# The last residual of a decode kernel moved from VectorE to TensorE and ScalarE

## The chip, the cores and the metric

The kernel runs on one core of one Trainium2 chip. The metric is the device time of one execution in microseconds (us). A profile of one execution shows, for each engine (PE is TensorE, PEld its weight loads, DVE is VectorE, ACT is ScalarE, POOL is GpSimd, SP is SyncE), what ran when. Its span reaches from the first to the last instruction of the program; the time of the execution is a little longer than the span.

## What is computed

One token goes through an attention block over a key and value cache and then through a small MLP block. Cut to what matters:

```
h   = x + attention(layernorm(x), k_cache, v_cache, wq) @ wo   # 32 heads, 8 key/value heads, 16384 keys of 128
b   = layernorm(h)
x1  = b + hs          # hs comes from h's neighbours 1 and 2 tokens away; with one token it is zero
out = h + x1 + gelu(layernorm(x1) @ w3) @ w4                   # w3: 512 x 1792, w4: 1792 x 512
```

So x1 is layernorm(h), and the result is 512 numbers in bf16. `h + x1` is the residual of the title; the kernel calls it `xsum`.

## The kernel before, in words

The work is written as a list of operations, each with the names that it reads and writes, and `Program` (L25) turns the list into instructions for each engine with semaphore waits between them. Every engine works off its operations in the order in which they are written. All large loads are issued by SP, and so they land in the order of their issue: `wq`, then keys and values of four pairs of heads (`kb`, `vb`), then `wo` in three pieces (`WO`, L359, rows 0-15, 16-27, 28-31 of its 32), `w3` in two pieces, and `w4` in four (`W4`, L362: of its 14 chunks 0-3, 4-8, 9-12 and 13).

A loop over the four pairs computes scores, softmax and the values' sums (L727 to L744). TensorE runs it as a real loop of instructions (`_tensor`, L158): its code is one copy of the body, with branches back. VectorE's code is written out in full (`_vector`, L143).

Behind the loop comes the tail, which the change touches:

- `o_b` (L760) is the attention's result. The 32 matmuls with `wo` follow (L766). Where the second piece of `wo` begins, at `r_ == 16`, stands `unread(4)`: one matmul of 128 x 512 whose output nobody reads, run four times in a loop on TensorE (L505; the loop's branch is at L338).
- The result goes through a sum over partitions, gets `x` added and becomes `hr`, which is `h` laid out over 128 partitions x 128 (the 32 partitions of block q all hold columns 128q to 128q+127). Row sums, variances and two inverse roots give the two layernorms' factors; one root runs on VectorE, the other on GpSimd.
- `hc` (L780, ScalarE) goes into the 16 matmuls with `w3` (L786), ScalarE takes Gelu (L798), VectorE transposes the result into `hcol` in two halves (L802).
- GpSimd makes `xs`, which is x1, and `xsum = hr + xs` (L793, L795).
- 14 chunks of four matmuls each (L810) multiply `hcol` by `w4` and add up in `n_ps[:, 0:128]`, a PSUM tile of 128 x 128 in fp32. The four matmuls of a chunk write the four strips of 32 partitions.
- VectorE adds `n_ps` and `xsum` into `fin`, in bf16 (L815). SP writes rows 0, 32, 64 and 96 of `fin`, 256 B each, to the output (L817) and waits for that (L819).

Two operations of the tail have no function, `dve(None, ...)` at L805 and `pe(None)` at L808. Each stands for a branch that never goes back (L154 and L344): VectorE waits until the second piece of `w4` has landed and then runs its branch; TensorE runs its branch after the fourth chunk of `w4`. For both a branch hint was marked at the start of the program (L146, L223). The code behind the branch is a block of its own (`ve_on`, `pe_on`).

`_tensor` writes each operation with `times` outside the main loop as a loop block of its own (L330 to L341): here that is `unread(4)` alone.

`ident_f` is a 128 x 128 identity in fp32, made at the start.

Of the kernel before, what the change touches and what calls it, by code (L numbers as in the profile page):

```python
# [9 lines left out]
ALU = mybir.AluOpType  # L10
ACTF = mybir.ActivationFunctionType
# [347 lines left out]
WO = ((0, 16), (16, 28), (28, 32))  # L359
VP = 2  # L360
W3 = ((0, 2), (2, 4))
W4 = ((0, 4), (4, 9), (9, 13), (13, 14))  # L362
# [13 lines left out]
def bass_sequential_preLN__gqa_block_cached__mixer_s_mlp__decode_kernel(  # L376
# [13 lines left out]
    with ExitStack() as ctx:  # L390
# [18 lines left out]
        ident_f = sb("ident_f", [128, 128], FP32)  # L409
# [35 lines left out]
        xsum = sb("xsum", [128, 128], FP32)  # L445
# [3 lines left out]
        fin = sb("fin", [128, 128], BF16)  # L449
# [13 lines left out]
        m_ps, n_ps = mn_ps[:, 0:256], mn_ps[:, 256:512]  # L463
# [28 lines left out]
        def dve(fn, r=(), w=(), bank=()):  # L492
            return P.op("DVE", fn, r, w, bank)

        def act(fn, r=(), w=(), bank=()):
            return P.op("ACT", fn, r, w, bank)
# [4 lines left out]
        def pe(fn, r=(), w=(), bank=(), also=()):  # L501

            return P.op("PE", fn, r, w, bank, also=also)

        def unread(times):  # L505
            field = qb[:, :, :, :].rearrange("p a j q -> p (a j q)")
            P.op("PE", lambda e: e.matmul(O_ps[1][:, :], field[:, 0:128], field[:, 0:512], start=True, stop=True),  # L507
                 r=["qb"], bank=[("O", 1)], times=times)

        def piece(cuts, m):  # L510
            return [lo <= m < hi for lo, hi in cuts].index(True)

        def copies(col, n):

            return col.to_broadcast([col.shape[0], n])
# [38 lines left out]
        def inverse_root(i, n, by, beside):  # L554
# [9 lines left out]
            for m in range(3):  # L564
# [22 lines left out]
            r=["ident", "x4"], w=["quarter"])  # L587
        pe(lambda e: e.matmul(O_ps[0][:, 0:128], quarter[:, :, :].rearrange("p q u -> p (q u)"), x4[:, :],  # L588
                              start=True, stop=True), r=["quarter"], w=[("O", 0)], bank=[("O", 0)])
# [9 lines left out]
            r=["ident_f"], w=["row32"])  # L599
        dve(lambda e: e.tensor_reduce(maskdd[:, :], ident_f[:, :].rearrange("p (n d) -> p d n", d=4), AX.X, ALU.add),  # L600
            r=["ident_f"], w=["maskdd"])
# [6 lines left out]
        for z, m, key, mk in ((zo, rowgh, "zo", "rowgh"), (zd, maskgh, "zd", "maskgh")):  # L608
# [5 lines left out]
            r=["hT", (("st", 0), 0), (("st", 0), 6)] + [("v", x) for x in range(VP)], w=["xn"])  # L614
# [3 lines left out]
        for i, key in enumerate(keys):  # L618
            P.part("query", i)
            for k in range(NCH):  # L620
                pe(lambda e, k=k: e.matmul(row[:, bass.ds(P.b + P.b0, 512)], copies(xn[:, k:k + 1], 128),  # L621
                                           wq_k[:, k, bass.ds(P.c + P.c0, REP * DH)], start=(k == 0), stop=(k == NCH - 1)),
                   r=["xn"], also=[("v", x) for x in range(VP)], w=["n" if key == "mn" else key], bank=[key])
        P.part()
        for g in range(2):
            half = banks[64 * g:64 * g + 64, PAIRS * g:PAIRS * g + PAIRS, :].rearrange("p j c -> p (j c)")
            for b in range(2):
# [3 lines left out]
                    r=["n" if x == "mn" else x for x in keys[PAIRS * g:PAIRS * g + PAIRS]], w=["qcol"],  # L631
                    bank=keys[PAIRS * g:PAIRS * g + PAIRS])
# [121 lines left out]
        for n, (lo, hi) in enumerate(W4):  # L754
# [4 lines left out]
            r=["o_m"], w=["o_f"])  # L759
        dve(lambda e: e.tensor_copy(o_b[:, :], o_f[:, :]), r=["o_f", ("r", 0, 0)], w=["o_b"])  # L760

        for r_ in range(32):
            q = r_ % 4
            if r_ == WO[1][0]:
                unread(4)
            pe(lambda e, r_=r_, q=q: e.matmul(O_ps[0][32 * q:32 * q + 32, :], copies(o_b[:, r_:r_ + 1], 32),  # L766
                                              wo_sb[:, r_ * D:(r_ + 1) * D], start=(r_ < 4), stop=(r_ >= 28)),
               r=["o_b"] + [("r", 0, n) for n in (piece(WO, r_),) if n], w=[("O", 0)], bank=[("O", 0)])
        h_ps, hkey = banks[:, 6, :], "spare0"
        for n in range(2):  # L770
            dve(lambda e, n=n: e.tensor_copy(osum[:, 256 * n:256 * n + 256], O_ps[0][:, 256 * n:256 * n + 256]),
                r=[("O", 0)], w=[("osum", n)], bank=[("O", 0)])
        for q in range(4):
            pe(lambda e, q=q: e.matmul(h_ps[32 * q:32 * q + 32, 0:128], copies(row32[:, 0:1], 32),
                                       osum[:, q * 128:(q + 1) * 128], start=True, stop=True),
               r=[("osum", q // 2), "row32"], w=[hkey], bank=[hkey])
# [4 lines left out]
            r=["hT", (S, 0)] + [("r", 1, 0)], w=["hc"])  # L781


        for k in range(NCH):
            for q in range(4):
                pe(lambda e, k=k, q=q: e.matmul(s_ps[32 * q:32 * q + 32, 0, 0:FQ], hc[:, k, :],  # L786
                                                w3_sb[:, k, q * FQ:(q + 1) * FQ], start=(k == 0), stop=(k == NCH - 1)),
                   r=["hc"] + [("r", 1, n) for n in (piece(W3, k),) if n], w=[("s", 0)], bank=[("s", 0)])
# [5 lines left out]
            r=["hr", (S, 0), (S, 6)], w=["xs"])  # L794
# [11 lines left out]
        for m in range(NHC):  # L806
            if m == W4[1][0]:
                pe(None)  # L808
            for o in range(4):
                pe(lambda e, m=m, o=o: e.matmul(  # L810
                    n_ps[32 * o:32 * o + 32, 0:128], hcol[:, m, :], w4_sb[:, m, o * 128:(o + 1) * 128],
                    start=(m == 0), stop=(m == NHC - 1),
                    skip_group_check=True),
                   r=[("hcol", 2 * m // NHC)] + [("r", 1, len(W3) + n) for n in (piece(W4, m),) if n], w=["n"], bank=["mn"])
        dve(lambda e: e.tensor_tensor(fin[:, :], n_ps[:, 0:128], xsum[:, :], ALU.add), r=["n", "xsum"], w=["fin"],  # L815
            bank=["mn"])
        P.op("SP", lambda e: e.dma_start(out[0, 0:1, :].rearrange("o (q j) -> (o q) j", q=4), fin[0:128:32, :]),  # L817
             r=["fin"], w=["out"], dma="out")
        P.op("SP", lambda e: e.nop(), r=["out"])  # L819
# [31 lines left out]
```

## Time and profile before

| | |
|---|---|
| median of 3 runs | 192.34 us (192.22 to 192.51) |
| profiled execution | 192.24 us |
| its span | 190.3 us |
| granted TensorE clock, mean of the span | 0.86 of full speed |
| busy in the span | TensorE 125.7 us, VectorE 117.9 us, ScalarE 9.2 us, GpSimd 7.4 us |
| read from memory | 79.17 MB, 416 GB/s over the span |

How to read it: in a group of instructions, `out<-in` are the program's names, `x36` a count, and times in brackets are idle time of that engine just before, with what ended it. "L810" is line 810 of the kernel. The chain that ended last goes back from the last instruction to what released each step. Of 190.3 us, DMA has 66% of that chain, VectorE 15% and TensorE 14%. Matmuls are pipelined, so their ends are modelled. PEclk is the granted clock of TensorE as a share of full speed.

### The profile page before, as it was taken

The page shows a single profiled execution, that of the slowest core. Times are in us where ns is not written, and L with a number is a line of the kernel's source. Part 1 is how long each engine was busy: PE and PEld are TensorE (multiplying, and loading weights), DVE is VectorE, ACT ScalarE, POOL GpSimd, SP SyncE. Part 2 cuts the span into 40 slices and gives each one's busy share as a digit, 9 for nine tenths or more (in the row PEclk, how much of TensorE's full clock was granted, in tenths as well). Part 3 has the DMA queues.
Part 4 walks back from the last instruction along what each step waited for, and adds up shares of the span by engine and source line. Part 5 has one row for each costly group of instructions (what it writes and reads, how often), then busy time and mean ns, then how long its engine had stood idle before and what let it go on. Part 6 is the DMA issues. An engine that isn't in the chain of part 4 may idle for free.

```text
span 190.3 us, 2315 instructions
## 1 busy us (share of the span) xinstructions
PE 125.7 (66%) x733; PEld 48.5 (25%) x733; DVE 117.9 (62%) x152; ACT 9.2 (5%) x16; POOL 7.4 (4%) x16
## 2 busy tenths in 40 slices
PE   0119709997770599964944989658359996865552
PEld 0103303442230233321311433213113332321131
DVE  6740799995523989845049989450479895522270
ACT  3000000000200000011000000020000000500030
POOL 7100000000000000000000000000000000000050
PEclk9999995899999579998585899996858999799755
DMA  6999999999999999997999999889999999999991
GB/s 221 441 441 441 441 441 441 441 441 441 399 413 420 420 551 441 441 441 331 441 441 441 551 399 399 386 379 420 441 441 441 441 441 441 441 386 395 423 408 46
DMA packets 3330, 79.20 MB, mean 416 GB/s; under 512 B 384, under 2 KB 512, under 8 KB 1280
## 3 DMA queue, kind: packets, MB, share of 16 engines
q1 hardware_dynamic: 3320, 79.17, 97.1%
q8 instruction: 1, 0.02, 0.0%
q14 instruction: 1, 0.01, 0.0%
q10 hardware_dynamic: 8, 0.00, 0.0%
HBM read 79.17 MB, written 0.00 MB: 416 GB/s over the span
## 4 chain that ended last, share of the span: by engine, by line
DMA 66%; DVE 15%; PE 14%; issue 2%; SPq 1%; DVEq 0%
DMA kb<-in_A_k_cache_dram 45%; DMA kb<-in_B_w_dram 14%; DVE kt L644 14%; PE banks L661 9%; DMA vb<-in_A_wq_dram 6%; PE banks L621 5%; SPq L467 1%; DVE qcol L628 1%; PE banks L655 1%; DVE qb L635 0%; PE banks L810 0%; DVE xn L612 0%; DVE fin L815 0%; SPq L139 0%; DVEq L139 0%
## 5 line engine op out<-in xcount | busy, mean ns | idle before, releaser
L644 DVE STREAM_TRANSPOSE kt<-kb 128x2048 int32<-128x2048 int32 (+1 forms) x37 | 71.3, 1989 | 6.9 <-DMA kb<-in_A_k_cache_dram 5.3
L661 PE MATMUL banks<-kt,qn 128*128 x256 | 68.9, 416 | 0.9 <-DVE kt L644 0.2
L661 PEld LDWEIGHTS banks<-kt,qn 128*128 x256 | 26.5, 104 | 41.4 <-issue 23.8
L697 PE MATMUL banks<-vb,pt 128*32 128x512 bf16 x256 | 19.2, 463 | 3.5 <-POOLq L482 3.0
L655 PE MATMUL banks<-qn 128*128 128x512 bf16 x8 | 4.0, 495 | 19.6 <-DVE kt L644 19.5
L713 DVE TENSOR_SCALAR od<-banks,rowc 128x128 f32<-128x128 f32 x4 | 1.4, 351 | 21.9 <-PE banks L697 21.9
L507 PE MATMUL banks<-qb 128*128 128x512 bf16 x40 | 14.3, 434 | 0.3
L686 DVE STREAM_TRANSPOSE pt<-p_sb 64x1024 bf16<-64x1024 bf16 x8 | 9.9, 1240 | 5.4 <-ACT p_sb L682 5.3
L621 PE MATMUL banks<-vb,xn 128*128 x32 | 9.0, 451 | 6.1 <-DVE xn L612 6.1
L682 ACT ACTIVATE p_sb<-banks,bias 128x1024 bf16<-128x1024 f32 x4 | 4.5, 1114 | 155.4 <-DVE nmh L678 155.4
L697 PEld LDWEIGHTS banks<-vb,pt 128*32 128x32 bf16 x256 | 7.6, 114 | 13.3 <-issue 5.6
L671 DVE TENSOR_REDUCE mx<-banks 128x1 f32<-128x1024 f32 x4 | 4.9, 1225 | 8.1 <-PE banks L661 8.1
L628 DVE STREAM_TRANSPOSE qcol<-banks 64x1024 f32<-64x1024 f32 x4 | 4.8, 1228 | 7.2 <-PE banks L621 7.2
L563 POOL TENSOR_SCALAR st<-st 128x1 f32<-128x1 f32 x1 | 0.2, 243 | 176.5 <-DVE st L543 176.5
L507 PEld LDWEIGHTS banks<-qb 128*128 128x128 bf16 x40 | 4.2, 107 | 9.3 <-issue 8.8
L655 PEld LDWEIGHTS banks<-qn 128*128 128x128 bf16 x8 | 0.8, 100 | 22.5 <-issue 22.3
L621 PEld LDWEIGHTS banks<-vb,xn 128*128 128x128 bf16 x32 | 3.6, 113 | 11.1 <-issue 8.6
L674 PE MATMUL banks<-mxd,mean 128*128 128x128 f32 x8 | 2.0, 332 | 6.6 <-DVE mxd L672 6.6
L719 PE MATMUL banks<-od,zo 128*32 128x128 f32 x8 | 1.6, 285 | 6.5 <-DVE od L716 6.5
L716 DVE SCALAR_TENSOR_TENSOR od<-banks,rowc,od 128x128 f32<-128x128 f32 x12 | 4.2, 351 | 0.4
L766 PE MATMUL banks<-kb,o_b 128*32 128x512 bf16 x32 | 2.5, 409 | 3.0 <-DMA kb<-in_A_wo_dram 1.8
L588 PE MATMUL banks<-x,quarter 4*128 4x128 bf16 x1 | 0.3, 285 | 6.0 <-DVE quarter L586 6.0
(77 smaller groups left out, 48.5 us busy)
## 6 DMA issues: line engine op xcount, KB each, us to landing
kb<-in_A_k_cache_dram SPq DMA_DIRECT2D x8, 4096.0 KB, 29.7
vb<-in_A_v_cache_dram SPq DMA_DIRECT2D x2, 4096.0 KB, 29.8
vb<-in_A_wq_dram SPq DMA_DIRECT2D x1, 4096.0 KB, 12.2
kb<-in_A_wo_dram SPq DMA_DIRECT2D x1, 2048.0 KB, 25.0
kb<-in_B_w_dram SPq DMA_DIRECT2D x2, 896.0 KB, 23.2
kb<-in_A_wo_dram SPq DMA_DIRECT2D x1, 1536.0 KB, 28.3
kb<-in_B_w_dram SPq DMA_DIRECT2D x2, 512.0 KB, 25.9
kb<-in_B_w_dram SPq DMA_DIRECT2D x1, 640.0 KB, 26.0
```

The lines of the kernel that those rows point to most:

```text
L507: P.op("PE", lambda e: e.matmul(O_ps[1][:, :], field[:, 0:128], field[:, 0:512], start=True, stop=True), r=["qb"], bank=[("O", 1)], times= ...
L621: pe(lambda e, k=k: e.matmul(row[:, bass.ds(P.b + P.b0, 512)], copies(xn[:, k:k + 1], 128), wq_k[:, k, bass.ds(P.c + P.c0, REP * DH)], sta ...
L628: dve(lambda e, g=g, b=b, half=half: e.transpose(qcol[64 * g:64 * g + 64, 2 * b:2 * b + 2, :, :].rearrange("p e m u -> p (e m u)"), half.r ...
L644: P.op("DVE", lambda e, view=view: e.transpose(view(kt), view(kb[y])), r=[("r", y, i) for i in range(RPARTS)], w=[("kt", t + i) for i in r ...
L655: pe(lambda e: e.matmul(row[:, bass.ds(P.y, 512)], copies(none, 128), copies(none, 512), start=True, stop=False, skip_group_check=True), r ...
L661: pe(lambda e, n=n: e.matmul(row[:, bass.ds(P.y, 512)], qn[:, n, bass.ds(P.q, 128)], key_piece(P.k, n), start=False, stop=(n == 3), skip_g ...
L671: dve(lambda e: e.tensor_reduce(mx[:, :], s_all, AX.X, ALU.max), r=[("s", 0), ("s", 1)], w=["mx"], **both)
L682: act(lambda e: e.activation(p_sb[:, :], s_all, ACTF.Exp, bias=bias[:, 0:1], scale=float(SCALE), accum_out=acc[:, :]), r=[("s", 0), ("s", ...
L686: dve(lambda e, g=g: e.transpose(pt[64 * g:64 * g + 64, :, :, g, :], p_sb[64 * g:64 * g + 64, :]), r=["p"], w=["pt"])
L697: pe(lambda e, l=l, ct=ct, ch=ch: e.matmul(O_ps[0][32 * ct:32 * ct + 32, :], pt[:, l, ch, :, :].rearrange("p g u -> p (g u)"), tiles[:, l ...
L716: dve(lambda e, block=block, c=c: e.scalar_tensor_tensor(od[:, :], block, rowc[:, c:c + 1], od[:, :], ALU.mult, ALU.add), r=[key, "rowc", ...
L766: pe(lambda e, r_=r_, q=q: e.matmul(O_ps[0][32 * q:32 * q + 32, :], copies(o_b[:, r_:r_ + 1], 32), wo_sb[:, r_ * D:(r_ + 1) * D], start=(r ...
```

## The change

The residual is no longer added by VectorE behind the last matmul. TensorE adds it: a matmul of the identity `ident_f` with `xsum`, in fp32, is written ahead of chunk 9 of `w4`, the first chunk of the third piece, and accumulates into the same PSUM tile. ScalarE then copies the tile into `fin`. VectorE's last operation is now its branch at L154. `unread(4)` is taken out, and with it the loop block between the 16th and 17th matmul with `wo`.

```diff
         for r_ in range(32):
             q = r_ % 4
-            if r_ == WO[1][0]:
-                unread(4)
             pe(lambda e, r_=r_, q=q: e.matmul(O_ps[0][32 * q:32 * q + 32, :], copies(o_b[:, r_:r_ + 1], 32),
...
         for m in range(NHC):
             if m == W4[1][0]:
                 pe(None)
+            if m == W4[2][0]:
+                pe(lambda e: e.matmul(n_ps[:, 0:128], ident_f[:, :], xsum[:, :], start=False, stop=False,
+                                      skip_group_check=True), r=["ident_f", "xsum"], w=["n"], bank=["mn"])
             for o in range(4):
                 pe(lambda e, m=m, o=o: e.matmul(
                     n_ps[32 * o:32 * o + 32, 0:128], hcol[:, m, :], w4_sb[:, m, o * 128:(o + 1) * 128],
...
-        dve(lambda e: e.tensor_tensor(fin[:, :], n_ps[:, 0:128], xsum[:, :], ALU.add), r=["n", "xsum"], w=["fin"],
-            bank=["mn"])
+        act(lambda e: e.activation(fin[:, :], n_ps[:, 0:128], ACTF.Identity), r=["n"], w=["fin"], bank=["mn"])
         P.op("SP", lambda e: e.dma_start(out[0, 0:1, :].rearrange("o (q j) -> (o q) j", q=4), fin[0:128:32, :]),
              r=["fin"], w=["out"], dma="out")
```

## The prediction

> **What bounds the kernel now.** I read the chain that ended last first, in order of time, because it says which wait is the last one.
>
> ```profile
> 159.67 26.82 DMA kb<-in_B_w_dram
> 186.50 0.04 issue
> 186.54 0.75 PE banks L810 x20
> 187.29 0.03 issue
> 187.32 0.29 DVE fin L815
> ```
>
> The columns are start, duration, what. The stream of weights holds everything up to 186.50 us; behind it stand 0.75 us of matmuls and one VectorE add. So what the change does before 186.5 costs nothing as long as TensorE is ready there. Next comes the timeline of the tail (start, duration, engine, line, and in brackets the idle time before and its releaser).
>
> ```profile
> 185.08 1.15 PE L810 MATMUL banks<-kb,hcol 128*32 128x128 bf16 x36 [1.29 <-DVE hcol L802]
> 185.42 0.46 POOL L795 TENSOR_TENSOR xsum<-hr,xs 128x128 f32<-128x128 f32 x1
> 186.54 0.72 PE L810 MATMUL banks<-kb,hcol 128*32 128x128 bf16 x20 [0.31 <-DMA kb<-in_B_w_dram]
> 187.32 0.29 DVE L815 TENSOR_TENSOR fin<-banks,xsum 128x128 bf16<-128x128 f32 x1 [1.82 <-PE banks L810]
> 187.64 0.62 SPq L817 DMA_DIRECT2D out_dram<-fin  x1
> ```
>
> The reader sees a gap of 0.31 us on TensorE ahead of the third piece of w4. `xsum` is ready at 185.88, early. After 187.64 only the output's DMA is left, and the span ends at 190.35. That end is worth a closer look: SP's own waits say
>
> ```profile
> SPq L819 <- DMA out_dram<-fin: 2.1, 1, 2.1
> ```
>
> 2.1 us for 1 KB. I therefore cut the end into stretches of 0.05 us (columns: stretch, length, busy time of five engines, clock, share of the DMA engines, GB/s), and looked at the queues on the page.
>
> ```profile
> 188.85:188.90 0.05, 0.00 (x0) 0.00 (x0) 0.00 (x0) 0.00 (x0) 0.00 (x0) 0.50 0.10 16
> ...
> 188.95:189.00 0.05, 0.00 (x0) 0.00 (x0) 0.00 (x0) 0.00 (x0) 0.00 (x0) 0.50 0.38 164
> ...
> 189.25:189.30 0.05, 0.00 (x0) 0.00 (x0) 0.00 (x0) 0.00 (x0) 0.00 (x0) 0.50 0.03 5
> ```
>
> ```profile
> q8 instruction: 1, 0.02, 0.0%
> q14 instruction: 1, 0.01, 0.0%
> ```
>
> Rate by length gives bytes. 16 GB/s x 0.05 us is 800 B: three of the output's four rows of 256 B, at 188.86 to 188.88. 164 x 0.05 is 8.2 KB: the one packet of queue 14, an instruction load of 8192 B; in the trace's packet records it runs from 188.97 to 189.28. 5 x 0.05 is 256 B: the fourth row, at 189.27, at the moment when that load ends. The output's semaphore rises at 189.24, 189.25 and 189.26 for three rows, and at **190.32** for the fourth. So an instruction load on the fourth row's DMA engine holds the end back by 190.32 - 189.26 = **1.06 us**. The Trainium skill, "DMA: Bandwidth & Descriptors", section "Queues, rings and completion order", says that a semaphore's increment lands only after every earlier write of that DMA engine, across its queues; by that rule the trace agrees, since the fourth increment comes 1.04 us after the load's end, and the other three about 0.37 us after their rows.
>
> Whose load is it? The engines' last instructions end at 184.78 (ScalarE), 185.89 (GpSimd), 187.29 (TensorE), 187.61 (VectorE) and 190.35 (SP). The load at 188.97 is 1.36 us after VectorE's end and 1.68 after TensorE's. Another 8192 B load stands at 191.66, 1.31 us after SP's end. The like distance makes **VectorE's end** the likeliest trigger; ScalarE and GpSimd show no 8192 B load behind their ends. Queue 8's load, 16 KB at 186.33, comes 1.1 us after the branches that TensorE (185.16) and VectorE (185.23) run, and disturbs nothing here.
>
> **The change part by part.** The profiled execution took 192.24 us, of which 190.35 are span; the 1.89 around it I keep. The median of the runs is 0.10 higher.
>
> (1) VectorE ends on its branch. The branch at L154 comes once the second piece of w4 has landed, and stands at 185.23 to 185.30. Today VectorE still waits behind it for `xsum` and the matmuls and ends at 187.61. Afterwards nothing follows the branch, so the same load should come at 185.30 + 1.36 = 186.66, 0.3 us behind the last row of weights (186.35) and about 2.3 us before the output's rows. It then meets neither. The fourth row goes out with the other three: **-1.06 us**. Bounds: 0 (load not VectorE's, or still late) and -1.06.
>
> (2) ScalarE copies instead of VectorE adding. The trace has no copy of 128x128 from PSUM on ScalarE. Nearest rows:
>
> ```profile
> L682 ACT ACTIVATE p_sb<-banks,bias 128x1024 bf16<-128x1024 f32 x4 | 4.5, 1114 | 155.4 <-DVE nmh L678 155.4
> L798 ACT ACTIVATE hg<-banks,st 128x224 bf16<-128x224 f32 x2 | 0.9, 490 | 1.6 <-DVE st L569 1.6
> L780 ACT ACTIVATE hc<-hT,st 128x128 bf16<-128x128 f32 x1 | 0.4, 401 | 17.1 <-DVE st L533 17.1
> L561 ACT ACTIVATE st<-st 128x1 f32<-128x1 f32 x1 | 0.2, 203 | 0.1
> ```
>
> From 224 to 1024 columns it is (1114 - 490)/800 = 0.78 ns a column. L561 is Identity with no operand for bias, as in the new line: 203 + 127 x 0.78 = 302 ns. L780, with a bias column, took 401. Against VectorE's 292 ns that is +0.01 to +0.11; I take **+0.02**, by the like form. No table load follows: Identity at L561 ran between the two Gelu uses with no load in between. Behind ScalarE's new wait for TensorE nothing but SP's DMA is queued.
>
> (3) TensorE adds `xsum`. One fp32 matmul of 128x128 by 128x128 is two weight loads and two passes. It lies in the 0.31 us gap ahead of the third piece. At the clock of the tail (0.50), the passes of L774 (fp32, 128 columns) start 0.216 us apart, and the weight loads of L531 (fp32, 128 columns) 0.165 apart. The first weight load can start when `xsum` is there and the ninth chunk's weights are in use, at about 185.92; the second lies beside the first pass: 0.165 + 2 x 0.216 = 0.60, to 186.52, against 186.54 for the third piece. That gives 0; I take **+0.05**, for switching between the whole array and its four column strips. The upper bound has no overlap: L531's whole pair took 0.59 with 2 columns, and 128 columns add about 0.1 to each pass (the groups of L810, 128 columns, follow every 0.107 us), so 0.80, less the gap of 0.31: +0.49. Below nothing it cannot go: the weights land when they land. The new wait for GpSimd is met at 185.89; behind it are the last 20 matmuls, and everything waits for these.
>
> (4) The four unread matmuls and their loop go. They lie at 174.29 to 175.33, and TensorE then waited 1.39 us for wo. What could change is the clock:
>
> ```profile
> 171.23:174.64 3.41, 1.74 (x20) 0.68 (x21) 1.29 (x5) 0.00 (x0) 0.00 (x0) 1.00 0.96 406
> 174.64:178.05 3.41, 1.58 (x20) 0.39 (x17) 0.00 (x0) 0.00 (x0) 0.00 (x0) 1.00 1.01 414
> 178.05:181.47 3.42, 2.10 (x14) 0.92 (x14) 1.69 (x8) 0.00 (x0) 0.00 (x0) 0.50 1.00 415
> ```
>
> The granted clock steps at these borders. After 1.74 us busy it stayed, after 1.58 it halved. Without the unread matmuls the first stretch has 1.74 - 0.28 = 1.46, so the clock may halve at 174.64 already. Then the 12 matmuls at 176.72 take three steps of about 0.43 in place of 0.216 (L766 took 379 ns full and 599 halved): the array is free at 178.01, and the last wo piece starts at 177.99 anyway. **+0.02**, all of it before the gap: 0 on the path. The Trainium skill, "TensorE: Matmul & The Clock Gate", section "HAM oscillation — how this bites in real kernels", speaks against this part: waits for DMA without filler send the clock to half, and the next matmuls start cold. By that rule the sum would be up to 0.02 us longer. The tail is at 0.50 with the filler already, so most of what it warns of is paid today.
>
> Sum: 192.24 - 1.06 + 0.02 + 0.05 = **191.25**; from the median 191.35. I say 191.3.
>
> **The rivals.**
> A. The load at 188.97 belongs to TensorE's end, or waits for the 16 KB load on queue 8 (186.33 to 187.73) and again falls on the output. For it: TensorE too ends shortly before. Against: 1.68 us does not match SP's 1.31. The gain is gone: 192.24 + 0.07 = 192.3.
> B. Slower: ScalarE's end takes VectorE's place and asks for a block like the one of queue 8, 16 KB in 1.40 us. ScalarE now ends with the output's DMA issue, so that load would hold the fourth row 1.40 - 0.31 = 1.09 us longer than today: 192.31 + 1.09 = 193.4. It decides if ScalarE's end needs a load at all; today none follows its end at 184.78.
> C. TensorE is late: no overlap, +0.49 in place of +0.05: 191.7.
> D. VectorE's early load meets the weights' last rows: if it started 0.3 us earlier, an increment of the last piece could come 1.06 us late, which gives the gain back: 192.3.
>
> **How the numbers follow.** Forecast 0.55 (191.0 to 191.6: 0.1 of run to run below, ScalarE's 0.11 and some of TensorE's price above), A 0.20, B 0.10, C 0.08, D 0.07. A measurement tells 0.2%, here 0.38 us, from no change. Faster: forecast and C, 0.63. A and D lie within it, except where C's price comes on top (192.3 + 0.4), 0.05: same 0.22. Slower: B and that, 0.15. The range of 191.0 to 192.5 holds forecast, C and most of A and D, about 0.83; B is left out.
>
> **What would show it.** Right: the instruction load of 8 KB near 186.7 and no load between the output's rows; SP's wait for the output near 1.0 us; `fin` on ScalarE near 0.30 us; TensorE's idle time before the third piece nearly gone, and its last matmul still ending near 187.3. Wrong: SP's wait still 2.1 us (A), or above 3 (B); the last 20 matmuls starting after 186.9 (C); the fourth piece of w4 waited for by a microsecond (D).

## The result, and the profile after

| | before | after |
|---|---|---|
| median | 192.34 us (7 runs, 192.08 to 192.57) | 191.14 us (7 runs, 191.00 to 192.01) |
| ratio | | 0.9947, 95% interval 0.9937 to 0.9957 |
| profiled execution | 192.24 us, span 190.3 | 192.01 us, span 190.6 |
| span of the other executions | 190.0 to 190.7 (in the experiments) | 189.7 to 190.0 |

The change is faster by 0.5%, as forecast. But the execution that was profiled is the odd one of the seven: it took 192.01 us, the six others 191.00 to 191.40. Its trace has to be read with that in mind, and it turns out to be the most telling of all. SP's wait for the output first (columns: engine, line, what it waited for, us in total, times, longest):

```profile
SPq L819 <- DMA out_dram<-fin: 2.0, 1, 2.0
```

It is still 2.0 us; the forecast had said 1.0. The page counts the instruction loads in the span, two now on queue 14 where there was one,

```profile
q8 instruction: 1, 0.02, 0.0%
q14 instruction: 2, 0.02, 0.0%
```

and short stretches find them (columns as before: stretch, length, busy time of five engines, clock, share of the DMA engines, GB/s).

```profile
186.75:186.80 0.05, 0.05 (x1) 0.00 (x0) 0.00 (x0) 0.00 (x0) 0.00 (x0) 0.50 0.45 164
189.15:189.20 0.05, 0.00 (x0) 0.00 (x0) 0.00 (x0) 0.00 (x0) 0.00 (x0) 0.50 0.07 10
189.20:189.22 0.02, 0.00 (x0) 0.00 (x0) 0.00 (x0) 0.00 (x0) 0.00 (x0) 0.50 0.09 13
189.22:189.24 0.02, 0.00 (x0) 0.00 (x0) 0.00 (x0) 0.00 (x0) 0.00 (x0) 0.50 1.16 410
189.55:189.60 0.05, 0.00 (x0) 0.00 (x0) 0.00 (x0) 0.00 (x0) 0.00 (x0) 0.50 0.02 5
```

Rate by length again: 164 x 0.05 is an 8 KB load at 186.78, 1.30 us after VectorE's last instruction (185.48). That is the load that was at 188.97; it was forecast for 186.66. Then 10 x 0.05 and 13 x 0.02 are three rows of the output, 410 x 0.02 is **another 8 KB load at 189.23**, and 5 x 0.05 is the fourth row, at 189.60, when that load ends. So VectorE's load left the place between the rows, and in this execution another one stood there. The tail's timeline:

```profile
186.15 0.80 PE L808 MATMUL banks<-xsum,ident_f 128*128 128x128 f32 x2
186.87 0.46 PEld L811 LDWEIGHTS banks<-kb,hcol 128*32 128x32 bf16 x20 [0.22 <-issue]
186.87 0.72 PE L811 MATMUL banks<-kb,hcol 128*32 128x128 bf16 x20
187.65 0.28 ACT L816 ACTIVATE fin<-banks 128x128 bf16<-128x128 f32 x1 [2.89 <-PE banks L811]
187.95 0.62 SPq L817 DMA_DIRECT2D out_dram<-fin  x1
```

ScalarE's copy takes 0.28 us, VectorE's add took 0.29. The residual's matmul starts at 186.15 and the third piece of w4 at 186.87 in place of 186.54, though its last semaphore increment came at 186.45. The time outside the span fell too, from 1.9 us to 1.4.

### The profile page after: what moved, and what is told of

Its sections match the earlier page's. It is cut to its first block, busy times and chain, and to the rows that moved or that the text cites. A ratio compares the mean times of both kernels' runs of the same rounds, so it can differ in the third digit from the quotient of the medians.

```text
span 190.6 us, 2302 instructions
## 1 busy us (share of the span) xinstructions
PE 125.2 (66%) x731; PEld 48.2 (25%) x731; DVE 117.6 (62%) x151; ACT 9.5 (5%) x17; POOL 7.4 (4%) x16
## 4 chain that ended last, share of the span: by engine, by line
DMA 66%; DVE 16%; PE 12%; issue 4%; ACT 0%; SPq 0%; DVEq 0%; ACTq 0%
DMA kb<-in_A_k_cache_dram 44%; DMA kb<-in_A_wo_dram 15%; DVE kt L644 13%; DMA vb<-in_A_wq_dram 6%; PE banks L621 5%; PE banks L661 4%; PE banks L764 1%; PE banks L811 1%; DVE qcol L628 1%; PE banks L772 1%; DVE st L567 0%; DVE qb L635 0%; PE banks L808 0%; PE banks L655 0%; PE banks L531 0%
## 5 line engine op out<-in xcount | busy, mean ns | idle before, releaser
L697 PE MATMUL banks<-vb,pt 128*32 128x512 bf16 x256 | 18.6, 453 | 3.5 <-POOLq L482 2.9
L507 PE MATMUL banks<-qb 128*128 128x512 bf16 x36 | 12.7, 387 | 0.3
L507 PEld LDWEIGHTS banks<-qb 128*128 128x128 bf16 x36 | 3.5, 96 | 8.8 <-issue 8.6
L704 PE MATMUL banks<-acc,zd 128*32 128x1 f32 x8 | 0.9, 186 | 5.3 <-DVE pt L686 5.3
```

Source lines behind the costliest of these rows:

```text
L697: pe(lambda e, l=l, ct=ct, ch=ch: e.matmul(O_ps[0][32 * ct:32 * ct + 32, :], pt[:, l, ch, :, :].rearrange("p g u -> p (g u)"), tiles[:, l ...
```

## The experiments

Three questions were open: whose load is the second one; is it really the held-back row that the change was paid for; and what does the residual cost on TensorE. Each run was timed beside the kernel before.

### The changed kernel once more: after_again

No edit.

> The changed kernel once more, unaltered, for a second profile. In the first one an instruction load of 8 KB stood at 189.23 us, between the output's rows, and that execution took 192.01 us while the six others took 191.0 to 191.4. Theory 1: the load is the second part of what VectorE's end asks for (2.4 to 2.7 us after the first), it is not tied to the output, and meets it only now and then: most runs 191.1, and a profile without a collision has a span of about 189.7 and SP's wait for the output near 1.0 us. Theory 2: the load is what ScalarE's end asks for (1.30 us after it), tied to the output's issue: then every run should meet it, and most runs would be near 192.0.

Twelve executions: seven at 190.93 to 191.35 us (spans 189.6 to 190.0) and five at 192.22 to 192.48 (spans 190.8 to 191.1); median 191.34, ratio 0.9965 (0.9946 to 0.9984). Its profile fell among the five: loads at 187.12 and 189.56, the fourth row at 189.89. Theory 2 falls, since most runs miss the collision. Theory 1 holds, though the collision is commoner than six to one. The changed kernel has **two kinds of executions**, near 191.1 and near 192.2. All profiles of it are of the second kind; the first is known by its times and spans, and by the kernels below. The third profile is after_third (191.99 us, loads at 186.88 and 189.30):

> The changed kernel unaltered, for a profile of an execution without a collision: span near 189.7 us, SP's wait near 1.0 us, execution near 191.1 us. One time in three it should show the collision again: 192.2.

### Only the filler taken out: no_filler

```diff
-            if r_ == WO[1][0]:
-                unread(4)
```

> The kernel before with the four unread matmuls and their loop taken out, nothing else. Theory: nothing on the path, 192.3 us (within 0.1 of the kernel before), and the instruction load still between the output's rows. Rival: the loop or the clock carries part of the gain; then 191.9 or less, or 192.6 or more.

192.24 us, ratio 1.0004 (0.9996 to 1.0013). The filler and its loop are worth nothing that can be seen here (0.13% at most). In its profile an 8 KB load stands at 188.84 and the fourth row at 189.32, 0.35 behind the third: held back as before.

### VectorE late again: vector_late

```diff
         act(lambda e: e.activation(fin[:, :], n_ps[:, 0:128], ACTF.Identity), r=["n"], w=["fin"], bank=["mn"])
+        dve(lambda e: e.tensor_tensor(xs[:, :], hr[:, :], hr[:, :], ALU.add), r=["n", "hr"], w=["xs"])
```

> The changed kernel with one more VectorE instruction behind its branch, an addition of 128x128 that waits for the last matmul and whose result nobody uses. VectorE then ends as late as in the kernel before, and nothing waits for it. Theory: the gain goes, since the load moves back between the output's rows and the time behind the span grows again: 192.4 to 192.7 us. Rival: the gain comes from the residual's new place or from ScalarE's copy; then it stays at 191.1.

192.74 us, ratio 1.0027 (1.0018 to 1.0036): the whole gain goes, and more. Nobody waits for this instruction; it only makes VectorE end at 188.22. So the gain comes from when VectorE ends; the residual's new place and ScalarE's copy bring none as long as VectorE ends late.

### Without the residual: no_residual

```diff
-            if m == W4[2][0]:
-                pe(lambda e: e.matmul(n_ps[:, 0:128], ident_f[:, :], xsum[:, :], start=False, stop=False,
...
```

> The changed kernel without TensorE's matmul of the identity with the residual: the residual is left out of the output. Theory: the third piece of w4 starts at 186.54 again in place of 186.87, the last matmul ends 0.33 us earlier: 190.8 us. Rival: the time is set elsewhere (the postamble of VectorE's end), 191.1.

190.60 us (190.51 to 190.95, five runs), ratio 0.9924 (0.9911 to 0.9936). This kernel leaves the residual out of its output. The third piece starts 0.04 us behind its last increment again, at 186.47. The output's rows now come before the second load:

```profile
186.75:186.80 0.05, 0.05 (x16) 0.05 (x8) 0.00 (x0) 0.00 (x0) 0.00 (x0) 0.50 0.45 164
188.75:188.85 0.10, 0.00 (x0) 0.00 (x0) 0.00 (x0) 0.00 (x0) 0.00 (x0) 0.50 0.07 10
189.20:189.25 0.05, 0.00 (x0) 0.00 (x0) 0.00 (x0) 0.00 (x0) 0.00 (x0) 0.50 0.59 164
```

```profile
SPq L816 <- DMA out_dram<-fin: 1.0, 1, 1.0
```

All four rows lie in 188.77 to 188.85 (10 GB/s x 0.10 us is 1 KB), and SP waits 1.0 us in place of 2.0. The profile also settles the second load. ScalarE ends 0.40 us earlier than in the changed kernel, at 187.53, and the load stays at 189.22: it is 2.45 us behind the first, as in the changed kernel (2.45), and not 1.30 behind ScalarE.

### VectorE a little later: vector_mid2 and vector_mid5

```diff
+        for n in range(2):        # 5 in vector_mid5
+            dve(lambda e, n=n: e.tensor_tensor(hx[:, :], (hx if n else hr)[:, :], hr[:, :], ALU.add),
+                r=["hr"] + ["hx"] * (n > 0), w=["hx"])
```

The additions stand behind the branch, and nobody uses them.

> The changed kernel with two VectorE additions of 128x128 behind its branch, which nobody waits for, so that VectorE ends about 0.63 us later. Theory: both instruction loads follow VectorE's end, at 187.4 and 189.85, the second behind the output's rows at 189.2: no run near 192, all near 191.1. Rival: the second load follows ScalarE's end: it stays at 189.23, and a third or more of the runs stay near 192.2.

191.07 us (six runs, 190.97 to 191.64), ratio 0.9940 (0.9926 to 0.9954), and none near 192. In the profile VectorE ends at 186.62 (1.13 us later than in the changed kernel; the weights landed 0.3 us later in this profile). Both loads moved with it, the second to behind the rows:

```profile
187.70:187.80 0.10, 0.10 (x12) 0.00 (x0) 0.00 (x0) 0.00 (x0) 0.00 (x0) 0.50 0.27 82
189.50:189.60 0.10, 0.00 (x0) 0.00 (x0) 0.00 (x0) 0.00 (x0) 0.00 (x0) 0.50 0.07 10
190.15:190.20 0.05, 0.00 (x0) 0.00 (x0) 0.00 (x0) 0.00 (x0) 0.00 (x0) 0.50 0.45 164
```

So the second load too is VectorE's.

> The same with five additions: VectorE ends about 1.6 us later, near 187.1. Both loads miss the output's rows (188.4 and 190.85). In the runs so far the semaphores of VectorE's closing work are reset 3.45 to 3.67 us after its end, or 0.35 to 0.38 us after SP's end, whichever is later. Theory: the former is later here, 190.55 + 0.2 against 190.0, so the time behind the span grows by about 0.55 us and the time is 191.6 to 191.8. Rival: the time behind the span is fixed: 191.1.

191.74 us (191.60 to 192.03), ratio 0.9970 (0.9960 to 0.9980). Here no load meets a row, and SP's wait and the span are as short as in the changed kernel's better runs:

```profile
span 189.8 us, 2307 instructions
```

```profile
SPq L822 <- DMA out_dram<-fin: 1.0, 1, 1.0
```

And yet the time is 0.6 us longer than theirs. Something behind the span waits for VectorE. The trace's record of semaphores (the counters by which engines wait for each other) shows what: after the program's end all semaphores are set back, one after another, over 0.6 to 0.9 us. The table takes one of them as a mark, number 120, near the middle of that series; the execution is over 0.88 us after it in most profiles. (The expectation above had counted to an earlier one of the series.)

| profile | VectorE's end | SP's end | reset of 120 | behind VectorE | behind SP | execution |
|---|---|---|---|---|---|---|
| before | 187.61 | 190.35 | 191.36 | 3.76 | 1.02 | 192.24 |
| no_filler | 187.69 | 190.22 | 191.22 | 3.53 | 1.01 | 192.10 |
| vector_late | 188.22 | 190.73 | 191.74 | 3.52 | 1.01 | 192.62 |
| vector_mid5 | 187.38 | 189.75 | 190.74 | 3.37 | 0.99 | 191.62 |
| two_outputs (next) | 187.69 | 189.61 | 191.19 | 3.50 | 1.59 | 192.07 |
| vector_mid2 | 186.62 | 189.96 | 190.40 | 3.78 | **0.43** | 191.27 |
| no_residual | 185.50 | 189.21 | 189.64 | 4.15 | **0.43** | 190.52 |
| after | 185.48 | 190.61 | 191.04 | 5.56 | **0.43** | 192.01 |

The table falls in two. Below, the reset is 0.43 us behind SP's end, always. Above, it is later than that, and 3.4 to 3.8 us behind VectorE's end.

The same record shows the wait itself. Ahead of the resets semaphore 2 rises once for each engine, in turn; which rise is whose is read from the times. VectorE's comes 3.0 to 3.5 us behind its end in all twelve profiles, whichever chain is the last one. SP's comes 0.12 us behind SP's end or 0.02 behind VectorE's rise, whichever is later, and the resets begin 0.13 us behind SP's. In the kernel before, VectorE's rise is at 190.97 and SP's at 191.00, though SP had ended at 190.35. In the changed kernel, VectorE's is at 188.79 and SP's at 190.73. ScalarE's comes only 0.11 us behind the end of its copy.

### The kernel before with two output DMAs: two_outputs

```diff
-        P.op("SP", lambda e: e.dma_start(out[0, 0:1, :].rearrange("o (q j) -> (o q) j", q=4), fin[0:128:32, :]),
-             r=["fin"], w=["out"], dma="out")
-        P.op("SP", lambda e: e.nop(), r=["out"])
+        rows = out[0, 0:1, :].rearrange("o (q j) -> (o q) j", q=4)
+        for n, by in enumerate(("SP", "ACT")):
+            P.op(by, lambda e, n=n: e.dma_start(rows[2 * n:2 * n + 2, :], fin[64 * n:64 * n + 64:32, :]),
+                 r=["fin"], w=[("out", n)], dma=f"out{n}")
+        P.op("SP", lambda e: e.nop(), r=[("out", 0), ("out", 1)])
```

> The kernel before with its output written by two DMAs of two rows each, one from SP and one from ScalarE's queue, nothing else; VectorE still ends at 187.6 us. If the four rows lie on four DMA engines and two rows on two of them, VectorE's load may no longer meet a row. Theory 1 (what the prediction said): the held-back row alone is worth 1.06 us, so without a collision 191.2 to 191.3. Theory 2 (from the run with five additions): two chains end the execution, the output's and VectorE's closing work, 3.3 to 3.7 us from VectorE's end; without the collision the second still ends at 190.9 to 191.1 in place of 191.28, and the time falls by 0.2 to 0.4 only, to 191.9 to 192.1. If the profile shows a row held back again, the run tells neither.

This is the run that decides. The collision is gone, and the span is 0.7 us shorter than before's, at 189.6:

```profile
span 189.6 us, 2312 instructions
```

```profile
SPq L821 <- DMA out_dram<-fin: 1.3, 1, 1.3
```

```profile
188.80:188.85 0.05, 0.00 (x0) 0.00 (x0) 0.00 (x0) 0.00 (x0) 0.00 (x0) 0.50 0.50 164
188.90:188.95 0.05, 0.00 (x0) 0.00 (x0) 0.00 (x0) 0.00 (x0) 0.00 (x0) 0.50 0.07 10
189.15:189.25 0.10, 0.00 (x0) 0.00 (x0) 0.00 (x0) 0.00 (x0) 0.00 (x0) 0.50 0.03 5
```

VectorE's load still comes first, at 188.81; then two rows near 188.93 and two near 189.20. Each row's increment comes 0.37 us behind the row, so none is held back.

But the time is 192.24 us, ratio **1.0004** (0.9995 to 1.0013). Theory 1 falls: in the kernel before, the held-back row cost nothing. Theory 2 has the mechanism right and the size too large: the reset of 120 stayed at 191.19, against 191.36 in the profile of before, and medians show no gain at all. SP ended at 189.61, but its rise of semaphore 2 came at 190.83 only, 0.02 us behind VectorE's.

### A cheaper residual: res_strips and res_bf16

```diff
# res_strips
-                pe(lambda e: e.matmul(n_ps[:, 0:128], ident_f[:, :], xsum[:, :], start=False, stop=False,
-                                      skip_group_check=True), r=["ident_f", "xsum"], w=["n"], bank=["mn"])
+                for o in range(4):
+                    pe(lambda e, o=o: e.matmul(n_ps[32 * o:32 * o + 32, 0:128], ident_f[:, 32 * o:32 * o + 32], xsum[:, :],
+                                               start=False, stop=False, skip_group_check=True),
+                       r=["ident_f", "xsum"], w=["n"], bank=["mn"])
# res_bf16: xsum in BF16, and a copy of ident_f in BF16 made at the start
+        dve(lambda e: e.tensor_copy(ident_b[:, :], ident_f[:, :]), r=["ident_f"], w=["ident_b"])
...
+                pe(lambda e: e.matmul(n_ps[:, 0:128], ident_b[:, :], xsum[:, :], start=False, stop=False,
+                                      skip_group_check=True), r=["ident_b", "xsum"], w=["n"], bank=["mn"])
```

> The changed kernel with TensorE's fp32 matmul of the residual cut into four strips of 32 columns of the identity, one for each strip of the output. In the changed kernel the one wide matmul started at 186.15 us, 0.2 after the ninth chunk's last issue, and pushed the last matmul back by 0.33. Theory: the wide weight load waits until the strips' matmuls are through; four narrow ones don't, and start near 185.95, so the third piece starts at 186.54 again: 190.7 to 190.8 us, and the output's rows at 188.85 are out of reach of VectorE's second load at 189.2, so no run near 192. Rival: the price is the fp32 passes themselves; then still 191.1, and two kinds of runs.

> The changed kernel with the residual and the identity in bf16 for TensorE's matmul (one weight load, one pass); the residual is rounded to bf16. Theory: 0.1 for the load and 0.11 for the pass from 186.15 end before 186.54, so the third piece starts with its landing: 190.7 us, one kind of run. Rival: changing between the whole array and the strips costs by itself; then the last matmul ends 0.1 to 0.3 later and 190.9 to 191.1.

res_strips took 191.04 us (190.86 to 191.39, ratio 0.9935, 0.9922 to 0.9948), res_bf16 190.79 (190.60 to 190.87, ratio 0.9917, 0.9905 to 0.9930), neither with a run near 192. First res_strips, then res_bf16, from their timelines:

```profile
186.27 0.64 PE L809 MATMUL banks<-xsum,ident_f 128*32 128x128 f32 x8
186.72 0.73 PE L813 MATMUL banks<-kb,hcol 128*32 128x128 bf16 x20
```

```profile
186.28 0.29 PE L810 MATMUL banks<-xsum,ident_b 128*128 128x128 bf16 x1
186.64 0.72 PE L813 MATMUL banks<-kb,hcol 128*32 128x128 bf16 x20
```

In both the third piece starts 0.04 us after its last increment (186.68 and 186.60), as in the kernel before (186.50 and 186.54). The residual's price is gone either way. In the strips' case the same fp32 passes ran, and they started 0.10 us behind the start of the last of the 36 matmuls ahead of them; the wide matmul of the changed kernel started 0.24 behind it (186.15, against 185.90). So 0.15 of the wide form's 0.37 us is its later start; the other 0.22 was not taken apart. (The wide bf16 matmul starts as late, 0.25 behind, but is short enough.) By its time alone (191.04, forecast 190.7 to 190.8) res_strips would speak for its rival. But its spans do not (median 189.45 us, res_bf16 189.4): of the 0.25 us between the two medians, 0.2 lies behind the span. In the profile of res_strips the last block of resets, semaphores 7 to 53, begins 0.72 us behind SP's rise of semaphore 2, in that of res_bf16 0.38 us; why was not found out. res_bf16 is the fastest version that computes everything, 0.35 us below the changed kernel's median, with the residual rounded to bf16.

## Why the prediction was right, and where it was not

The number was right (191.3 for 191.14), and so was the trigger: VectorE's end. The reason given was not, so the closeness of the number is luck.

1. **VectorE's end, -1.06.** Right: the load between the rows was VectorE's, and it moved to 186.78 (forecast 186.66, counted from the branch at 185.30; VectorE's last transposition ends later, at 185.50 before and 185.48 after). Wrong: that the held-back row is what the execution waits for. two_outputs freed the row and gained nothing. The step that failed is "the 1.89 around it I keep": in the better runs of the changed kernel it is 1.3 to 1.5 us. In the kernel before, VectorE's closing work puts the mark, the reset of 120, at 191.36, 3.76 us behind VectorE's last instruction; by the output's chain alone, with the row held back, it would have come at 190.35 + 0.43 = 190.78. The row had 0.58 us of slack. The change takes VectorE's end from 187.61 to 185.48 and its rise of semaphore 2 from 190.97 to 188.79, and then the output's chain is the last: with SP's end at 189.7 in the better runs the mark comes at 190.1, 1.2 us earlier than 191.36. That this lies near 1.06 less ScalarE's and TensorE's terms is an accident of two sums. Without TensorE's price the change is worth 1.5 us (res_bf16, 190.79 against 192.30 beside it), more than the bound of 1.06 allowed.
2. **The row does count afterwards.** With the output's chain last, a held-back row costs all of it: 192.2 against 191.1. The forecast had VectorE's load out of the way and did not look for a second one. Before, it was there to be seen: the load at 191.66, read as SP's because it came 1.31 us after SP's end, is VectorE's second, 2.69 us behind the first. Moved with VectorE's end it comes to 189.2, next to the rows. By their times it met them in 7 of 20 executions of the changed kernel (7, 12 and 1); the three that were profiled all show it.
3. **ScalarE, +0.02.** 0.28 us for 0.29: -0.01. The like form (no operand for bias) was the right row; L780's 0.40 was not. ScalarE's end brought no load with it, so rival B had no footing. What the term left out is that ScalarE has next to nothing to close: 0.11 us, where VectorE has 3.0 to 3.5.
4. **TensorE, +0.05.** The term was mis-sized: +0.33 at the last matmul (rival C had +0.49 at its bound). The assumption that the first weight load starts at 185.92, beside the strips' matmuls, failed; it started at 186.15. no_residual at 190.60 shows that the price reaches the end of the better runs, where they take 191.1; the trace accounts for 0.37 of that 0.5.
5. **The filler, 0 on the path.** Right: no_filler 1.0004. The clock did fall a window earlier, as worked out, at 175.31 in place of 178.04:

```profile
171.89:175.31 3.42, 1.21 (x18) 0.33 (x16) 0.90 (x3) 0.00 (x0) 0.00 (x0) 1.00 0.97 410
175.31:178.72 3.41, 1.90 (x16) 0.41 (x16) 0.09 (x1) 0.00 (x0) 0.00 (x0) 0.50 0.99 404
```

After 1.21 us of work in 3.42 the clock halved, the matmuls with the second and third piece of wo took 1.90 us in one stretch, and still VectorE's copy behind them began at 178.63 (before: 178.64).

## What to carry to other kernels

Ask of every engine when it ends, not only of the last instruction: an engine that has nothing to do any more may still have closing work of microseconds, and where that ends last, moving its last instruction to an engine that closes sooner is worth more than the instruction. When the time outside the span is not the same in two kernels, something behind the span is on the path, and the span alone misleads; here it fell by 0.7 us for nothing in one kernel. And when a kernel has two kinds of executions, look at several before reading one profile.

## What the runs showed of the hardware

- VectorE's end was followed by two instruction loads of 8 KB on queue 14, the first 0.98 to 1.36 us behind it and the second 2.42 to 2.69 behind the first, in all twelve profiles. An instruction added to VectorE moves both.
- A load of 0.31 to 0.49 us on the DMA engine of a 256 B row held that row's semaphore back by 0.8 to 1.1 us (before: 1.06; no_filler: 0.83; vector_late: 0.86; after: 0.99): the row waits for the load's end, and its increment came 0.85 to 1.02 us after the row in place of 0.32 to 0.38.
- Behind the program each engine raised semaphore 2, and then all semaphores were set back. VectorE's rise came 3.0 to 3.5 us behind its end, SP's 0.12 and ScalarE's 0.11 behind theirs where no earlier rise was late; the resets began 0.13 us behind SP's. The Trainium skill, "Runtime: NRT & Kernel Launch", section "The ~15µs preamble/postamble breakdown", names a barrier over all engines and a reset of the semaphores behind a kernel, with about 1.5 us each; the order agrees with the trace, while the resets took 0.6 to 0.9 us here. Why VectorE needs 3.0 to 3.5 us was not taken apart; its first load lies in that time.
- An fp32 matmul of the whole array did not begin beside matmuls on strips of 32 columns as early as one cut into the same strips did: 0.24 us against 0.10 behind the start of the last of them.
